# Attention, SoLU and softplus on one core: all later loads of q, k and v issued from ScalarE's queue, under a new order of operations

## The chip, the core and the metric

The kernel runs on one core of a Trainium2 chip. The metric is device microseconds, the median of several executions; lower is better. Instructions are issued by five engines, each in its own program order: TensorE (PE, with PEld for its weight loads), VectorE (DVE), ScalarE (ACT), GpSimd (POOL) and SyncE (SP). SP does no arithmetic: in the kernel before, it issues every transfer between memories.

## The reference

Three stages follow one another. An attention over 4 batches, 8 heads, 576 positions and a head size of 64, where heads 0 to 3 see a window of 32 and heads 4 to 7 see 32 positions at a distance of 4; a first layer of 512 by 1024 by 512 with a SoLU and a normalisation between its two products; a second layer of 512 by 2048 by 512 with a softplus.

```python
scores = scale * np.matmul(q, k.transpose(0, 1, 3, 2))          # masked by window or dilation
attn = softmax(scores);  x = (attn @ v) as [2304, 512]
h = x @ w_in;  solu = h * softmax(h);  ln = (solu - mean) / sqrt(var + 1e-6) * g_ln
x = ln @ w_out
h = x @ w2_in;  out = softplus(h) @ w2_out
```

## The kernel before

All inputs are float32. Most products are made from a float16 high part and a float16 low part of each operand, three products instead of one; weights and activations are therefore split on ScalarE and VectorE (a high part `...h`, a low part `...l` or `...o`) before TensorE can use them.

The attention is cut into 28 pairs of blocks (`pair`, line 886): seven for each batch, of two kinds. The first ten (`NF = 10`, handled by `pair32`) are computed in float32 with their transposes on TensorE. The other eighteen, pairs 10 to 27, which I call the later pairs, are split into float16 parts, and everything that has to be turned is turned by transfers: `qT` and `kT` (q and k), `pT` (the probabilities, needed by the product with v, `PV`), `xT` (the attention output). `lnT` does the same for the normalised rows of the first layer. These transfers are `dma_t`, line 581. The plain loads are `dma`, line 578: a later pair of the dilated kind has three (`ld11.0`, `ld11.1`, `ld11.2` for q, k, v), one of the windowed kind six (`ld10.00`, `ld10.01` for q, `ld10.10`, `ld10.11` for k, `ld10.20`, `ld10.21` for v), 78 for all of them. They go into the buffers `rq`, `rk` and `rv`, which have one to three slots each, some of them lying in the tile `E`. A load can start when the pair that had the slot before has been split (`ql`, `kl`, `vl` on VectorE are the last to read it).

The order of all work is written out. The body of the program creates 2923 operations (`P.op`), each with the engines that may run it (`opts`); the list `ORDER` (line 191) names them in the order in which they are emitted, and `SLOTS` gives each buffer its slot. Every instruction is pinned to that order on its engine (`pin`, line 548). An entry below zero stands for a filler: one matrix product of constants into an idle bank, 512 columns wide, that nobody reads (`mm`, line 569, on the tile `eye`). The engine comes from this line of `order` (line 104):

```python
o.on = next(iter(o.opts)) if len(o.opts) == 1 else "DVE" if x >= n else "ACT"
```

Here `x` is the entry of the list and `n` is 2923. An operation with one possible engine runs there. One with two runs on ScalarE unless its entry has 2923 added to it. At the end of the program the operations are emitted one after the other by `o.fn(o.on)` (line 1883). When ScalarE passes from an exponential to a softplus or back, a load of its function table goes ahead (line 1882).

The pairs overlap with the other stages: by the trace the first layer's product of the first rows (`m1a0`) starts at 47 us, the first hidden product of the second layer (`h0.0`) at 124 us, the last pair ends at about 465 us, and from then on the second layer alone remains.

Of the kernel before, what the change touches and what calls it, by code (L numbers as in the profile page):

```python
# [134 lines left out]
def dma_cost(issue, land):  # L135
    return {"SP": (issue, land)}


def moving(packets, size, lag=2.05):

    return 1.05 * packets * (12 + size / 21.0) / 16000, lag
# [3 lines left out]
def kernel(  # L145
# [12 lines left out]
    nc = tc.nc  # L158
# [4 lines left out]
    HH = H // 2  # L163
# [413 lines left out]
    def dma(out, in_):  # L577
        pin(nc.sync.dma_start(out=out, in_=in_))
# [1335 lines left out]
```

## Time and profile before

| | |
|---|---|
| median of 3 runs | 687.52 us (685.85 to 689.7) |
| the profiled execution | 686.92 us |
| its span, first to last instruction | 685.2 us |
| PE busy | 665.7 us (97%) |
| DVE busy | 616.8 us (90%) |
| ACT busy | 490.5 us (72%) |
| transfers issued by SP | 217 plain, 126 turning |
| fillers in the list | 165 |

A busy PE is not one at its peak: matrix products are pipelined, and fillers count as busy too. The engines' shares are means over stages that differ; the stretches in the rows below tell them apart.

### The profile page before, as it was taken

What the parts mean: (1) busy time and instruction counts of PE and PEld (TensorE: products, weight loads), DVE (VectorE), ACT (ScalarE), POOL (GpSimd) and SP (SyncE); (2) the same over time, 40 slices, a digit from 0 to 9 for tenths busy, and PEclk for the clock granted to TensorE, in tenths of its full rate; (3) what the DMA queues carried; (4) which work ended last, traced back from release to release, by engine and by line L of the source; (5) the groups of instructions that cost most, each with busy time, mean ns of one, the idle gap of its engine ahead of it and who ended that gap; (6) DMA issues with size and microseconds to landing.
All of it is one profiled execution on the core that took longest, in us unless ns stands there. A gap on an engine that the chain in (4) does not pass through costs nothing.

```text
span 685.2 us, 14857 instructions
## 1 busy us (share of the span) xinstructions
PE 665.7 (97%) x5462; PEld 482.0 (70%) x5462; DVE 616.8 (90%) x1770; ACT 490.5 (72%) x1022; POOL 3.5 (1%) x22
## 2 busy tenths in 40 slices
PE   6999999999999999999999999999999999999997
PEld 4666557767875587777567757765758786788886
DVE  4999999999999878888889898888899999998997
ACT  5899998999998678755989669855544255553553
POOL 2000000000000000000000000000000000000000
PEclk9999999999999999999999999999999999999999
DMA  9999997788675669997878887753121200000000
GB/s 269 254 254 257 250 232 187 149 163 192 173 149 142 182 188 202 217 166 143 139 143 154 161 145 153 110 105 74 32 47 27 52 1 1 32 1 2 33 32 32
DMA packets 186776, 89.84 MB, mean 131 GB/s; under 512 B 157000, under 2 KB 174416, under 8 KB 186704
## 3 DMA queue, kind: packets, MB, share of 16 engines
q1 hardware_dynamic: 186704, 88.90, 58.6%
q8 instruction: 43, 0.70, 0.4%
q14 instruction: 29, 0.24, 0.1%
HBM read 54.53 MB, written 4.72 MB: 86 GB/s over the span
## 4 chain that ended last, share of the span: by engine, by line
PE 76%; DVE 9%; DMA 7%; ACT 4%; issue 2%; SPq 1%; DVEq 0%; ACTq 0%
PE bank L569 32%; PE ps_w L569 25%; PE bank L1688 11%; PE ps_w L1605 7%; DMA E<-in_moe_w_in_dram 2%; DVE W L560 2%; DMA pT<-p 2%; PE bank L575 1%; DMA W<-in_moe_w_out_dram 1%; ACT W L551 1%; ACT E L551 1%; DMA W<-in_moe_w_in_dram 1%; DVE osb L560 1%; ACT s L551 1%; DVE E L560 1%
## 5 line engine op out<-in xcount | busy, mean ns | idle before, releaser
L569 PEld LDWEIGHTS <-W 128*128 128x128 f16 x1824 | 176.6, 98 | 24.2 <-DMA lnT<-hl 1.5
L569 PE MATMUL ps_w<-W,g 128*128 128x512 f16 x576 | 130.4, 379 | 0.0
L569 PE MATMUL bank<-y,W 128*128 128x256 f16 x960 | 109.9, 273 | 0.0
L569 PE MATMUL bank<-lnT,W 128*128 128x256 f16 x864 | 98.8, 273 | 1.4 <-DVE rs L566 1.4
L569 PE MATMUL ps_w<-W,xr 128*128 128x512 f16 x432 | 98.0, 379 | 0.0
L569 PEld LDWEIGHTS <-g 128*128 128x128 f16 x576 | 55.4, 98 | 60.5
L569 PEld LDWEIGHTS <-xr 128*128 128x128 f16 x432 | 41.8, 98 | 45.4
L1688 PEld LDWEIGHTS <-W 128*128 128x128 f16 x528 | 51.7, 98 | 7.5
L1882 ACT ACT_TABLE_LOAD x39 | 50.0, 1283 | 0.7
L551 ACT ACTIVATE s<-s 96x128 f32<-96x128 f32 (+3 forms) x144 | 43.6, 374 | 8.7 <-DVE s L557 8.5
L551 ACT ACTIVATE E<-E 128x768 f32<-128x768 f32 (+2 forms) x48 | 35.9, 749 | 12.9 <-DMA E<-in_q_dram 5.1
L560 DVE SCALAR_TENSOR_TENSOR g<-r,KR,g 128x512 f16<-128x512 f32 (+1 forms) x57 | 40.9, 719 | 0.9 <-ACT g L551 0.7
L1136 DVE CUSTOM_DVE_ANT_0 s<-bank,band,bsc 96x128 f32<-96x128 f32 (+3 forms) x144 | 38.9, 323 | 1.7 <-PE bank L569 1.6
L569 PE MATMUL ps_w<-eye 128*128 128x512 bf16 x125 | 34.1, 379 | 0.0
L551 ACT ACTIVATE g<-r,KR 128x512 f16<-128x512 f32 (+1 forms) x41 | 28.2, 690 | 7.3 <-PE ps_w L1605 3.7
L551 ACT ACTIVATE hl<-e,st 128x1024 f16<-128x1024 f32 x18 | 22.3, 1238 | 14.9 <-DVE st L560 11.9
L551 ACT ACTIVATE r<-bank,invC 128x512 f32<-128x512 f32 x40 | 27.1, 684 | 7.8 <-DVE g L560 3.7
L569 PEld LDWEIGHTS <-eye 128*128 128x128 bf16 (+2 forms) x185 | 17.9, 104 | 16.7 <-POOL eye L627 4.0
L569 PEld LDWEIGHTS <-pT 128*96 128x96 f16 (+3 forms) x432 | 22.6, 123 | 7.2 <-DMA pT<-p 3.1
L560 DVE SCALAR_TENSOR_TENSOR E<-E 128x512 int32<-128x512 int32 x40 | 26.9, 684 | 0.2
L1605 PE MATMUL ps_w<-W,g 128*128 128x256 f16 x180 | 25.5, 273 | 0.6 <-DVE osb L560 0.6
L551 ACT ACTIVATE xf<-bank,rs 80x64 f32<-80x64 f32 (+1 forms) x100 | 22.9, 316 | 4.3 <-DVE rs L566 3.9
(368 smaller groups left out, 1306.6 us busy)
## 6 DMA issues: line engine op xcount, KB each, us to landing
E<-in_moe_w_in_dram SPq DMA_DIRECT2D x17, 512.0 KB, 4.8
E<-in_moe_w_out_dram SPq DMA_DIRECT2D x17, 512.0 KB, 4.1
out_dram<-osb SPq DMA_DIRECT2D x18, 256.0 KB, 2.6
W<-in_moe_w_in_dram SPq DMA_DIRECT2D x7, 512.0 KB, 5.6
W<-in_moe_w_out_dram SPq DMA_DIRECT2D x7, 512.0 KB, 4.8
E<-in_v_dram SPq DMA_DIRECT2D x9, 384.0 KB, 4.4
E<-in_q_dram SPq DMA_DIRECT2D x9, 384.0 KB, 4.1
E<-in_k_dram SPq DMA_DIRECT2D x9, 384.0 KB, 4.0
```

Of the source, the lines that this page charges most:

```text
L551: pin(nc.scalar.activation(out=out, in_=in_, func=func, **kw))
L560: pin(nc.vector.scalar_tensor_tensor(out=out, in0=in0, scalar=s, in1=in1, op0=op0, op1=op1, **kw))
L569: pin(nc.tensor.matmul(out, l, r, start=start, stop=stop))
L575: pin(nc.tensor.transpose(out, in_, eye32[:in_.shape[0], :in_.shape[0]]))
L1136: pin(nc.vector.tensor_tensor_reduce(out=sv()[:rows, h, :nk], in0=sb.t[:rows, h, :nk], in1=band[:rows, 48 - m:48 - m + nk], scale=sc[:rows ...
L1605: pin(nc.tensor.matmul(mi[q](), gt.t[:, a, ff, 128 - 128 * t:256 - 128 * t], b(w), start=start and x == 0, stop=x == 2, skip_group_check=True,
L1688: pin(nc.tensor.matmul(ps.t[:, ff, :], at(w, cc, ff), yo.t[:, v, cc, :], start=start, stop=cc == 1 and x == 2, skip_group_check=True,))
L1882: pin(nc.scalar.preload_act_table_set(TABLES[tab]))
```

## The change

Three edits. `dma` gets a third argument and issues on ScalarE's queue when that is "ACT", on SyncE's otherwise. The loads of pairs that are not `whole`, the later pairs, get a second possible engine, "ACT", and pass their engine on. `ORDER` and `SLOTS` are replaced by new lists. Transfers that turn (`dma_t`) and all other loads and stores stay on SyncE's queue.

```diff
     ORDER = (
-        64, 65, 237, -2, 240, 3164, 238, -2, 242, 243, -2, -2, 244, 245, 268, 267, 246, 0, 13, 256, 3, 14, 15, 16,
...
-    def dma(out, in_):
-        pin(nc.sync.dma_start(out=out, in_=in_))
+    def dma(out, in_, eng="SP"):
+        pin((nc.scalar if eng == "ACT" else nc.sync).dma_start(out=out, in_=in_))
...
-                        dma(buf.t[:cnt].rearrange("p (h r d) -> p h r d", h=HH, r=2), s)
+                        dma(buf.t[:cnt].rearrange("p (h r d) -> p h r d", h=HH, r=2), s, e)
...
-                    f"ld{n}.{x}", dma_cost(0.45, 2.35), load, uses=[buf], mv=moving(4 * cnt, 512),
+                    f"ld{n}.{x}", dma_cost(0.45, 2.35) if whole else {**dma_cost(0.45, 2.35), "ACT": (0.45, 2.35)}, load, uses=[buf], mv=moving(4 * cnt, 512),
...
-                        dma(to, s)
+                        dma(to, s, e)
...
-                    two.append(P.op(f"ld{n}.{x}{o}", dma_cost(0.45, 2.35), load, uses=[buf], mv=moving(4 * cnt, 256)))
+                    two.append(P.op(f"ld{n}.{x}{o}", dma_cost(0.45, 2.35) if whole else {**dma_cost(0.45, 2.35), "ACT": (0.45, 2.35)}, load, uses=[buf], mv=moving(4 * cnt, 256)))
```

The change is described as moving sixteen loads. Read from the code it moves 78: with two engines in `opts` a load runs on ScalarE unless its entry is 2923 or more, and no load of a later pair has such an entry in the new list. Counted from the lists: fillers fall from 165 to 148, loads of a function table on ScalarE rise from 39 to 43, and 119 splits and copies that either engine can do change sides, 59 from ScalarE to VectorE and 60 back.

## Rows read from the trace of the kernel before

**Rows 1.** Page, part 1: busy time, share of the span, instructions.
```profile
PE 665.7 (97%) x5462; PEld 482.0 (70%) x5462; DVE 616.8 (90%) x1770; ACT 490.5 (72%) x1022; POOL 3.5 (1%) x22
```

**Rows 2.** Windows: length, then PE, PEld, DVE, ACT, POOL busy, PEclk, DMA share, GB/s.
```profile
25.00:125.00 100.00, 96.56 (x749) 62.16 (x747) 97.67 (x271) 93.69 (x274) 0.00 (x0) 1.00 0.91 233
125.00:250.00 125.00, 123.78 (x966) 85.93 (x964) 116.13 (x341) 112.74 (x227) 0.00 (x0) 1.00 0.73 168
250.00:450.00 200.00, 196.19 (x1733) 141.70 (x1731) 171.00 (x623) 156.00 (x299) 0.00 (x0) 1.00 0.83 157
450.00:675.00 225.00, 224.41 (x1815) 174.61 (x1813) 211.04 (x485) 112.18 (x180) 0.00 (x0) 1.00 0.14 32
...
275.00:300.00 25.00, 24.78 (x219) 18.06 (x218) 20.64 (x79) 16.70 (x33) 0.00 (x0) 1.00 1.00 194
```

**Rows 3.** Waits of PE from 125 to 455 us: total, times, longest.
```profile
PE bank L569 <- DMA kT<-E: 1.4, 1, 1.4
PE bank L569 <- DVE s L1136: 1.3, 2, 1.1
PE bank L569 <- DVE E L560: 1.2, 1, 1.2
PE bank L569 <- DVE xf L563: 0.8, 2, 0.5
PE bank L569 <- DMA pT<-p: 0.3, 1, 0.3
```

**Rows 4.** Chain that ended last, 324 to 340 us: start, length, what.
```profile
328.98 1.07 SPq L581
...
330.21 2.85 DMA pT<-p
...
337.90 0.85 DVE s L1136 x7
```

**Rows 5.** The same chain, 396 to 406 us.
```profile
398.11 2.01 SPq L581
...
400.52 3.68 DMA kT<-E
```

**Rows 6.** Timeline of SP, 324.7 to 350.4 us; 21 transfers in all.
```profile
324.72 1.68 SPq L581 DMA_TRANSPOSE E<-qk  x1
...
328.16 0.57 SPq L578 DMA_DIRECT2D rv<-in_v_dram  x1
...
330.21 1.21 SPq L581 DMA_TRANSPOSE pT<-p  x1
...
335.61 1.90 SPq L578 DMA_DIRECT2D E<-in_v_dram  x1
337.56 1.55 SPq L581 DMA_TRANSPOSE qT<-E  x1
...
349.93 0.50 SPq L578 DMA_DIRECT2D E<-in_q_dram  x1
```

**Rows 7.** Line 578, the plain transfers: ns min/median/max of an issue, first and last.
```profile
L578 SPq DMA_DIRECT2D rk<-in_k_dram x27: 328/480/1227, 1.7 to 401.9; - x27
L578 SPq DMA_DIRECT2D rv<-in_v_dram x19: 378/526/1331, 39.7 to 450.3; - x19
```

**Rows 8.** Timeline of ACT, 147 to 150 us.
```profile
147.76 0.62 ACT L551 ACTIVATE E<-E 128x512 bf16<-128x512 f32 x1
```

**Rows 9.** Chain, 147 to 149 us.
```profile
148.03 0.02 ACTq L551
...
148.50 5.94 DMA E<-in_moe_w_in_dram
```

**Rows 10.** Groups by line: busy us, mean ns, idle before.
```profile
L1882 ACT ACT_TABLE_LOAD x39 | 50.0, 1283 | 0.7
...
L551 ACT ACTIVATE s<-s 96x128 f32<-96x128 f32 (+3 forms) x144 | 43.6, 374 | 8.7 <-DVE s L557 8.5
...
L569 PE MATMUL ps_w<-eye 128*128 128x512 bf16 x125 | 34.1, 379 | 0.0
...
L551 ACT ACTIVATE g<-r,KR 128x512 f16<-128x512 f32 (+1 forms) x41 | 28.2, 690 | 7.3 <-PE ps_w L1605 3.7
```

**Rows 11.** Timeline of PE, 99 to 108 us: fillers, and the end of the front.
```profile
102.50 1.46 PE L569 MATMUL bank<-eye 128*128 128x512 bf16 x6
...
107.11 1.16 PE L569 MATMUL bank<-lnT,W 128*128 128x256 f16 x9 [1.39 <-DVE rs L566]
```

**Rows 12.** Chain, 98 to 126 us.
```profile
98.78 6.04 DMA E<-in_moe_w_in_dram
...
124.13 1.97 PE bank L569 x18
```

383 rows, old and new, of tables (ORDER, SLOTS) are left out of this document.

## The prediction, made before the change was run

> **What bounds the kernel now.** I read the shares of the page first [rows 1]: TensorE is busy 97% of the span, VectorE 90%, ScalarE 72%. These are means over stages, so I went to the stretches [rows 2]. TensorE's granted clock is 1.00, the 2.4 GHz level, in each of them, so no term below is a clock term. From 450 us on TensorE is busy for 224.41 of 225 us with matrix products alone: nothing that the change does can shorten that stage. From 25 to 125 us VectorE (97.67 of 100) and ScalarE (93.69) are both full with splitting weights, the transfer engines stand at 0.91, and TensorE's 96.56 is partly filler. From 250 to 450 us, the stage of the later pairs, VectorE has 171 of 200 us, ScalarE 156, so ScalarE has 44 us free there, but 112.74 of 125 us in the stretch before.
>
> Then the waits of TensorE between 125 and 455 us [rows 3]. They add up to 1.4 + 1.3 + 1.2 + 0.8 + 0.3 = 5.0 us. That is all the plain idle time which a better feed of the later pairs could give back. To see whether SyncE's queue is behind it I followed the chain that ended last. At 328.98 us it goes through 1.07 us in which SyncE is the one that is late, then through the turning of the probabilities (2.85 us to landing) into the softmax work of VectorE at 337.90 us [rows 4]; at 398.11 us it goes through 2.01 us of SyncE and then the turning of k, 3.68 us [rows 5]. The queue is nearly full: from 324.72 to 350.43 us I add up the issues of 21 transfers to 23.2 us of 25.7, 90% [rows 6]. The nine plain loads among them take 7.3 us, 28% of the time; a turning transfer that is ready has to wait for whatever stands before it, and one load alone (335.61 us) stood for 1.90 us. So the direction of the change is right: SyncE's queue limits the turning transfers, and they are on the path.
>
> **The change part by part.** *SyncE loses 78 issues.* At the medians of 480 and 526 ns [rows 7], about 0.5 us each, that is 39 us, of which 57 loads, 28 us, lie after 250 us (counted in the trace). By the chain, 1.4 + 1.3 us of the waits hang on SyncE being late; the 0.8 and 0.3 us wait for probabilities that were turned or for what follows them. The 1.2 us follows VectorE's work on a weight that landed 5.94 us after its issue [rows 9], and stays. So 3.8 us can be reached. I take 2.5 of them, nearer to all than to none, since the loads' 28% of the queue's time comes free, but not all, since the transfers take 2.85 and 3.68 us to land by themselves and the 16 transfer engines are at 0.83 in the mean and 1.00 from 275 to 300 us [rows 2]. Bounds: 0 and 5.0 us.
>
> On that last point the Trainium skill, "DMA: Bandwidth & Descriptors", section "Issuing engines are not separate DMA queues", says that transfers issued by different engines run on the same 16 DMA engines and interleave, and that issuing from several saves only the issue time. By that rule only the two places where the chain names SyncE itself would improve; the trace agrees in so far as the landing takes longer there than the lateness of the queue.
>
> *ScalarE gains 78 issues.* No load is issued by ScalarE in the trace of before, so I bound the cost. From above: each takes 0.5 us of ScalarE as it does of SyncE, 39 us in all, 28 of them after 250 us. From below: nothing, because ScalarE's sequencer goes on while the engine works: at 148.03 us it executes a semaphore instruction [rows 9] in the middle of an operation that runs from 147.76 to 148.38 us [rows 8]. An issue of 0.5 us then lies beside the operation ahead of it, and those take 0.37 us (one head's exponential) to 0.69 us [rows 10]. A gain below nothing is excluded: nothing leaves ScalarE's queue. I take 0.15 us each, near the lower end, because the operations around the loads are mostly of the longer kind: 9 us after 250 us. To this come four more table loads, 4 x 1.283 = 5.1 us [rows 10]. Together 14 us, into 44 us of free time: 0 on the path. If that cover is gone, they cost their full length; that is a rival below. A load that waits for its slot holds every ScalarE operation behind it, the exponentials and splits of the next blocks, and through them VectorE and TensorE. Counted in the new list, 66 of the 73 loads that follow another pair in their slot have at least 1.5 us of VectorE's work between the release and the load, half of them over 8 us; so I price this wait at 0, with up to 1.5 us for seven of them, some 5 us if all fell on the path.
>
> *The front.* By the place of `h0.0` the new list has 16 fillers fewer. Six of them in a row take 1.46 us, so one goes by in (1.46 - 0.38) / 5 = 0.22 us [rows 10, 11], and 16 are 3.5 us. This is no gain by itself: fillers stand where TensorE has nothing else to do. At 107.11 us TensorE waits 1.39 us for VectorE [rows 11], and VectorE for the landing of a weight, 6.04 us after its issue [rows 12]. The bytes to be moved and the work of VectorE, which is full, are unchanged in sum (summed over both lists with the durations of the trace, VectorE's work ahead of the last split before `h0.0` agrees to within 1 us), and seven loads with 3.5 us of issue go to ScalarE, which has 6 us free in this stretch. I take 0, with bounds of 3.5 us less and 3 us more. The second half of the kernel, after 450 us, gets 0: its order changes, but TensorE has no gap to lose.
>
> *Sum.* -2.5 (turning transfers) + 0 (ScalarE) + 0 (front) + 0 (tail) = -2.5 us on the span of 685.2 us, 682.7 us. The profiled execution took 686.92 us, 1.7 us beyond its span, which makes 684.4 us; the median of the runs shown, 687.52 us, is 0.6 us above that execution. So I forecast 685.0 us, 0.4% less.
>
> **The rivals.** *A. ScalarE becomes late (slower).* Each load holds ScalarE's sequencer not for 0.5 us but until SyncE's current transfer has been issued, and the operations behind it run late. In the stretch of 25.7 us the 12 turning transfers take 15.9 us [rows 6], 62% of the time, and one takes 1.2 to 1.7 us. If the two queues issue one at a time, a load is held by up to 1.2 us on top of its own 0.5, and the cover of 0.4 to 0.7 us ahead of it no longer reaches. The point from which this decides: 57 loads share 44 - 5 = 39 us of free time after 250 us, 0.68 us each. At 0.8 us beyond the cover the stage grows by 57 x 0.12 = 7 us and the 2.5 us are not gained either: 694 us. For it speaks that ScalarE is already at 93 to 94 of 100 us in the first stretch and 90% in the second; against it that its sequencer runs ahead [rows 8, 9] and that it has the time.
>
> The skill, "Perfetto Trace Analysis", section "DMA Instruction — HWDGE (DVE, Sync)", says that the unit which generates descriptors is locked for exclusive use by one instruction, that the sequencer waits for the lock, and that the semaphore wait too is served by the sequencer. That is this rival's mechanism. No trace with one issuing queue can show the lock.
>
> *B. The front shortens as well (faster).* If all of the 5.0 us goes and the 16 fillers do mark time that TensorE no longer waits in, 687.5 - 5.0 - 3.5 = 679 us. For it: the chain runs through SyncE in the middle. Against: VectorE's 97.67 of 100 us.
>
> *C. Nothing moves.* The turning transfers still land late, because the transfer engines at 0.83 to 1.00 are the limit and not the queue, and ScalarE covers its issues: 687.5 us, give or take 1. The same comes out if the change did not do what it says; if only sixteen loads moved, SyncE would lose a fifth of the 39 us, and the gain would be 0.5 us.
>
> **How the numbers follow.** My forecast has a chance of 0.42 and a range of its own of 682 to 688 us. A has 0.27, B 0.16, C 0.15. Half a per cent, 3.4 us, is about what a measurement of this kernel can tell from no change: below 684.1 is faster, above 691 slower. Of the forecast 0.17 falls below 684.1 and 0.25 within; B is all faster; C within but for 0.01; A slower but for 0.02. That makes faster 0.33, same 0.41, slower 0.26. For 8 in 10 the range must take in most of A and half of B: 680 to 693.5 us, leaving out about 0.08 below and 0.1 above.
>
> **What the profile of the changed kernel would show.** Right: 78 issues on ScalarE's queue of about 0.5 us, most of them while an operation of ScalarE runs; SyncE no longer in the chain between 300 and 450 us; waits of TensorE between 125 and 455 us of about 2.5 us; ScalarE at 165 to 175 of 200 us in the stretch 250 to 450. For A: issues on ScalarE of over 1 us, idle time of ScalarE ended by "issue" or by its own queue, and waits of TensorE and VectorE for exponentials and splits. For B: `h0.0`, now at 124.13 us [rows 12], before 121 us. For C: the same waits, now for transfers alone. The prediction is wrong if an issue on ScalarE costs more than 0.68 us beyond its cover, if the front moves by more than 3 us either way, or if the new order opens gaps after 450 us.

## The result, and the profile after

The changed kernel takes 697.0 us in the median (695.3 to 698.2), the kernel before beside it 687.5: 1.0140 times as long, with an interval of 1.0116 to 1.0164, or 9.6 us. The forecast was 685.0 us, its range ended at 693.5. The profiled execution took 696.4 us with a span of 693.2. I follow the loss by the starts of the same operations in both traces.

The page after, busy time and transfer queues (packets, MB, share of 16 engines' span; q1 is SyncE's, q10 ScalarE's):

```profile
PE 666.6 (96%) x5445; PEld 481.2 (69%) x5445; DVE 617.6 (89%) x1769; ACT 497.2 (72%) x1042; POOL 3.5 (1%) x22
...
q1 hardware_dynamic: 151792, 77.43, 51.2%
q10 hardware_dynamic: 34912, 11.47, 8.6%
```

The change does what it says, and more than the sixteen loads of its name: 78 transfers, 11.47 MB, are on ScalarE's queue. ScalarE works 6.7 us longer than before [rows 1], of which four more table loads are 5.1; the other engines work as long as before, and TensorE, which ends last, is not kept by more work. The time is in waits.

The windows of after, columns as in [rows 2]:

```profile
25.00:125.00 100.00, 93.07 (x701) 58.57 (x699) 93.54 (x264) 89.19 (x262) 0.00 (x0) 0.97 0.86 224
...
105.00:110.00 5.00, 3.32 (x12) 1.36 (x13) 5.00 (x19) 5.00 (x20) 0.00 (x0) 0.56 0.94 212
110.00:115.00 5.00, 5.00 (x38) 4.01 (x37) 3.50 (x11) 2.99 (x9) 0.00 (x0) 0.75 0.46 131
125.00:250.00 125.00, 119.07 (x913) 80.61 (x913) 114.01 (x340) 109.44 (x220) 0.00 (x0) 1.00 0.76 160
250.00:450.00 200.00, 197.21 (x1736) 143.75 (x1733) 174.25 (x617) 158.98 (x308) 0.00 (x0) 1.00 0.88 163
450.00:675.00 225.00, 224.53 (x1820) 173.78 (x1818) 207.77 (x478) 118.30 (x199) 0.00 (x0) 1.00 0.16 33
```

Beside [rows 2] TensorE is busy 3.5 us less up to 125 us, 4.7 us less from 125 to 250, 1.0 us more in the stage of the later pairs, and as long as before behind 450 us. Busy time counts fillers, and 16 of them fewer are 3.5 us by the prediction's own price, so the first figure is no measure of a delay. The two windows from 105 to 115 us were, before:

```profile
105.00:110.00 5.00, 3.61 (x32) 2.83 (x31) 5.00 (x15) 4.86 (x15) 0.00 (x0) 1.00 1.03 261
110.00:115.00 5.00, 5.00 (x40) 3.41 (x39) 4.54 (x16) 3.35 (x11) 0.00 (x0) 1.00 0.41 120
```

The granted clock there, 1.00 before, is 0.56 and 0.75 after: part of that stretch at the lower level, 1.2 GHz. By the starts of operations the kernel is 4.3 us late at `h0.0` (128.26 us against 123.97), 9.2 us late at the matrix product for the weights of quarter 2 (191.07 against 181.90), and 8.2 us late from 438 us to the end.

The waits of TensorE after, 125 to 455 us (total, times, longest), beside [rows 3]:

```profile
PE bank L569 <- DMA qT<-qk: 3.7, 1, 3.7
PE bank L569 <- DMA kT<-qk: 1.4, 1, 1.4
PE bank L569 <- ACT r L551: 1.0, 2, 0.6
PE bank L569 <- ACT E L551: 1.0, 2, 0.8
PE bank L569 <- DMA pT<-p: 0.8, 2, 0.5
```

With 0.6 us more for `xf` that is 8.5 us instead of 5.0, and turning transfers lead the list. The chain that ended last shows the same places (start, length, what):

```profile
101.67 7.54 DMA lnT<-hl
109.25 4.35 PE bank L569 x24
...
136.71 8.10 DMA qT<-qk
...
153.33 8.79 DMA qT<-qk
162.16 3.79 PE bank L569 x42
170.34 8.50 DMA kT<-qk
```

Before, no turning transfer stood in the chain for more than 3.7 us where I had read it [rows 4, 5], nor for more than 5.0 elsewhere, and none at all between 95 and 205 us; here four take 7.5 to 8.8 us from issue to landing. (Standing in the chain is not a loss by itself: in e1 below, which loses next to nothing, turning transfers stand there for 24.1 us between 95 and 205 us.) What goes on beside the last of them is in the timelines of SP and ACT, 166 to 174 us:

```profile
169.03 1.26 SPq L581 DMA_TRANSPOSE qT<-qk  x1
170.34 2.60 SPq L581 DMA_TRANSPOSE kT<-qk  x1
```

```profile
169.74 0.39 ACTq L578 DMA_DIRECT2D rk<-in_k_dram  x1
171.77 0.45 ACTq L578 DMA_DIRECT2D rk<-in_k_dram  x1
172.37 1.00 ACTq L578 DMA_DIRECT2D rq<-in_q_dram  x2
```

The four loads of pair 13 go out on ScalarE's queue beside the two turnings of pair 12: the first 0.7 us behind that of q, the last within 3 us behind that of k, for which TensorE waits 1.4 us. (The wait of 3.7 us is for the turning of q at 153.33 us.) In the kernel before, three of these four loads stood behind both turnings in SyncE's queue (166.66 to 167.76 us, the turnings at 162.23 and 163.55), and the turnings landed after 3.7 and 4.2 us.

### The profile page after: what moved, and what is told of

It is laid out like the page before. It is cut to its first block, busy times and chain, and to the rows that moved or that the text cites. A ratio compares the mean times of both kernels' runs of the same rounds, so it can differ in the third digit from the quotient of the medians.

```text
span 693.2 us, 14857 instructions
## 1 busy us (share of the span) xinstructions
PE 666.6 (96%) x5445; PEld 481.2 (69%) x5445; DVE 617.6 (89%) x1769; ACT 497.2 (72%) x1042; POOL 3.5 (1%) x22
## 3 DMA queue, kind: packets, MB, share of 16 engines
q10 hardware_dynamic: 34912, 11.47, 8.6%
## 4 chain that ended last, share of the span: by engine, by line
PE 69%; DMA 14%; DVE 8%; ACT 7%; issue 2%; ACTq 0%; SPq 0%; DVEq 0%
PE bank L569 27%; PE ps_w L569 23%; PE bank L1688 10%; PE ps_w L1605 8%; DMA pT<-p 3%; DMA qT<-qk 2%; DVE W L560 2%; DMA E<-in_moe_w_out_dram 2%; DMA rq<-in_q_dram 1%; ACT E L551 1%; DMA kT<-qk 1%; DMA lnT<-hl 1%; DMA E<-in_v_dram 1%; DMA W<-in_moe_w_out_dram 1%; PE bank L575 1%
## 5 line engine op out<-in xcount | busy, mean ns | idle before, releaser
L551 ACT ACTIVATE E<-E 128x768 f32<-128x768 f32 (+3 forms) x49 | 36.4, 743 | 11.0 <-DMA E<-in_q_dram 3.1
L560 DVE SCALAR_TENSOR_TENSOR g<-r,KR,g 128x512 f16<-128x512 f32 (+1 forms) x53 | 37.9, 718 | 3.0 <-ACT g L551 2.8
L569 PE MATMUL ps_w<-eye 128*128 128x512 bf16 x117 | 32.7, 387 | 0.0
L551 ACT ACTIVATE xf<-bank,rs 80x64 f32<-80x64 f32 (+1 forms) x120 | 27.4, 315 | 3.7 <-DVE rs L566 3.5
L569 PE MATMUL bank<-kT,qT 128*80 128x112 f16 (+7 forms) x336 | 22.7, 235 | 5.2 <-DMA qT<-qk 3.7
L569 PEld LDWEIGHTS <-eye 128*128 128x128 bf16 (+2 forms) x168 | 16.4, 105 | 15.5 <-POOL eye L627 4.0
```

What stands on the lines that cost most here:

```text
L551: pin(nc.scalar.activation(out=out, in_=in_, func=func, **kw))
L560: pin(nc.vector.scalar_tensor_tensor(out=out, in0=in0, scalar=s, in1=in1, op0=op0, op1=op1, **kw))
L569: pin(nc.tensor.matmul(out, l, r, start=start, stop=stop))
```

## The experiments

Three theories. **Contention**: on a queue of their own the loads run beside the turning transfers on the same 16 transfer engines, and these land later. **Order**: the new list costs the time, whatever queue the loads are on. **ScalarE**: the issue holds ScalarE (rival A). The kernel before ran beside each kernel; "+" is the ratio's excess times 687 us.

| run | median us | ratio, 95% interval | us |
|---|---|---|---|
| changed list, all loads on SyncE (e1) | 687.0 | 0.9996 to 1.0045 | +1.4 |
| old list, all 78 on ScalarE (e2) | 692.2 | 1.0059 to 1.0111 | +5.8 |
| old list, pairs 10 to 13 on ScalarE (e6) | 693.5 | 1.0080 to 1.0127 | +7.1 |
| old list, pairs 14 to 27 on ScalarE (e4) | 687.9 | 1.0003 to 1.0039 | +1.4 |
| old list, pairs 10 to 13 on ScalarE, half of each load (h2) | 689.9 | 1.0021 to 1.0070 | +3.2 |
| old list on SyncE, 78 small issues on ScalarE (e5) | 687.7 | 0.9997 to 1.0029 | +0.9 |
| changed, five loads back on SyncE (e8) | 690.7 | 1.0038 to 1.0092 | +4.5 |
| changed, pairs 10 to 13 back on SyncE (a1) | 688.7 | 1.0007 to 1.0070 | +2.6 |
| changed, once more, two executions (a2) | 695.7 | 1.0085 to 1.0197 | +9.7 |

**Order or queue.** e1 keeps the changed list and undoes the queue; e2 keeps the old list and does the queue alone.

```
e1   def dma(out, in_, eng="SP"):
-        pin((nc.scalar if eng == "ACT" else nc.sync).dma_start(out=out, in_=in_))
+        pin(nc.sync.dma_start(out=out, in_=in_))
e2   dma(), load and options as in the changed kernel; ORDER and SLOTS of the kernel before
```

> The changed list with all 78 loads issued on SyncE again, so that only the order differs from the kernel before. Three theories. Order: the new list by itself loses the time (later weight loads, fewer fillers, clock at 0.50 near 105 to 112 us), whatever queue the loads are on: 695 to 699 us, h0.0 near 128 us, and the PE wait of 3.7 us on qT near 160 us still there. Contention: loads on a second queue run beside the turning transfers and make these land later: 689 to 692 us, because the losses after 128 us (about 5 us) go and only the first 4.3 us stay; the median landing of qT between 125 and 205 us goes back from 7.6 us to about 5.8. ScalarE: holding ScalarE for the issue costs the time: 689 to 692 too, but with the landing times unchanged.

> The order of the kernel before, with all 78 loads of q, k and v of pairs 10 to 27 on ScalarE's queue, so that only the queue differs from the kernel before. Order: no loss, 685 to 688 us, the PE waits of 125 to 455 us at 2.5 to 5.0. Contention: 691 to 696 us, qT's median landing between 125 and 205 us near 7.6 us instead of 5.8 and PE waits of several us on qT and kT there, h0.0 still near 124. ScalarE: 691 to 696 with landings as before and ScalarE's idle time ended by issue.

The changed list on SyncE takes 687.0 us and cannot be told from the kernel before: the order by itself costs at most 3.1 us (1.0045), and the order theory falls. The old list with the loads on ScalarE loses 5.8 us; its `h0.0` is 3.3 us late, where I had expected it near 124 us. Between e1 and the changed kernel only the queue differs, and that is 8.2 us. The waits of TensorE in e1, 125 to 200 us, have the 3.7 us on `qT` down to 0.8 and none on `kT`:

```profile
PE bank L569 <- DMA qT<-qk: 0.8, 1, 0.8
PE bank L569 <- ACT E L551: 0.7, 1, 0.7
```

I had expected e1 at 689 us or more, with the first 4.3 us of loss left in it; it had 2.0 at `h0.0` and gave them back later.

**ScalarE.** e5 lets ScalarE issue 78 transfers of 32 bytes where e2 had the loads, which stay on SyncE.

```
     pin(nc.sync.dma_start(out=out, in_=in_))
+    if eng == "ACT":
+        r = next(taken_rows)
+        pin(nc.scalar.dma_start(out=scratch[r:r + 1, :], in_=q[0, 0, r:r + 1, 0:8]))
```

> The kernel before, unchanged in order and with all loads on SyncE, and beside it 78 small transfers of 32 bytes on ScalarE's queue at the places in the list where the old-list run had the loads: ScalarE pays the issues, next to no bytes move. ScalarE theory (holding ScalarE costs the time): 690 to 693 us, as the old list with the loads on ScalarE (692.2). Contention theory (the loads' own packets beside the turning transfers cost it): 686 to 688.5 us, the turning transfers landing as in the kernel before.

```profile
L582 ACTq DMA_DIRECT2D scratch<-in_q_dram x78: 208/209/1161, 40.0 to 451.7; - x78
```

The issues (the row gives ns min/median/max) cost 0.9 us, 2.0 at the end of the interval; e2 lost 5.8 with as many issues and the bytes. These issues are shorter than a load's; three of the loads' groups in the changed kernel's trace are:

```profile
L578 ACTq DMA_DIRECT2D rv<-in_v_dram x19: 319/391/1187, 40.4 to 435.7; - x19
L578 ACTq EVENT_SEMAPHORE  x19: 17/17/3745, 95.1 to 418.3; - x19
L578 ACTq DMA_DIRECT2D rk<-in_k_dram x18: 319/386/516, 95.2 to 411.1; - x18
```

So a load holds ScalarE's sequencer for 0.39 us, less than the 0.48 and 0.53 us on SyncE [rows 7]. One load of 78 waited for its slot, 3.7 us at 313.1 us; ScalarE stood idle for 3.3 us behind it, and TensorE didn't wait there. Rival A falls as the cause of the 9.6 us; that issues as long as a load's cost a little more than e5's is not excluded.

**Which loads.** e6 and e4 split the old list's 78 loads; a1 and e8 take loads of the changed kernel back to SyncE at the same places. (An entry of the list above 2922 selects an operation's second option, for a load SyncE.)

```
e6, e4   ORDER of before, with entry -> entry + 2923 for the loads that stay on SyncE
a1       ORDER of after, entry -> entry + 2923 for the 18 loads of pairs 10 to 13
e8       1210 -> 4133, 1273 -> 4196, 1274 -> 4197, 1275 -> 4198, 1276 -> 4199
```

> The order of the kernel before, with the loads of pairs 10 to 13 alone on ScalarE's queue and those of pairs 14 to 27 on SyncE: the complement of the run with the late pairs, which lost 1.5 us. If the losses add up and lie mostly in the stretch where weight loads fill the engines, 690 to 691.5 us (4.4 us lost), lnT1 landing in over 7 us and the clock falling near 105 to 115 us; the stretch from 250 us on as before. If the loss is spread over all loads alike (22 of 78 here), 688 us.

> The order of the kernel before, with the loads of pairs 14 to 27 alone on ScalarE's queue, pairs 10 to 13 still on SyncE. Nothing ahead of about 200 us changes. Contention that costs only where SyncE's queue is full of weight loads and turning transfers: the front as before, the middle stage (250 to 450 us) 1.0 to 2.5 us shorter, 685 to 686.5 us. Contention that costs everywhere: pT and kT between 285 and 460 us land 0.4 to 1.0 us later and the time is 688 to 690 us. ScalarE: 688 to 692 us with ScalarE's busy share in 250 to 450 us at 165 or more of 200. Order alone: 687 us, no change.

> The changed kernel with the loads of pairs 10 to 13 (22) on SyncE at the same places of the list, those of pairs 14 to 27 still on ScalarE. Contention: all loads on SyncE took 687.0 us, all on ScalarE 697.0; the old list lost 7.0 us by the early loads and 1.5 by the late ones, the spliced list 2.75 by the late ones, so 688.5 to 690 us here, and 7 to 8.5 of the 10 us come back. If the late loads cost the changed list as much as the early ones: 692 us.

> The changed kernel with five of its 78 loads (ld12.1 and the four of pair 13 that follow qT12 and kT12) issued on SyncE at the same places of the list. Contention theory: qT11 (landing 8.8 us) and kT12 (8.5 us) were late because these loads ran beside them; the losses between 150 and 195 us (about 5 us) go, w2o2m begins 4 to 5 us late instead of 9.2, and the time is 691.5 to 693.5 us. If the turning transfers are late there for another reason (the weight loads ahead of them on SyncE): 696 to 698 us. ScalarE theory: five issues fewer, 0.3 us at most, 696 to 697 us.

Pairs 10 to 13 have 18 loads, six for each of the two windowed pairs and three for each of the two dilated; the expectations of a1 and h2 say 22, which is a miscount. These 18 early loads carry the loss: +7.1 alone on the old list (693.5 us, where I had expected 690 to 691.5), and taken back they bring the changed kernel from +9.6 to +2.6. Five of them make 5.1 of these 7.0. The 60 late ones cost 1.4 us, where I had hoped for a gain of 1.0 to 2.5. The parts don't add up exactly (7.1 + 1.4 against 5.8 for both). The intervals of e6 and e2 overlap; that a delay made early takes up part of one made later would also do it, and is not shown. In e8 the waits of TensorE from 125 to 200 us are:

```profile
PE bank L569 <- DMA qT<-qk: 1.5, 1, 1.5
PE bank L569 <- ACT E L551: 0.6, 1, 0.6
```

The wait on `kT` is gone with the four loads of pair 13, that on `qT` is down by 2.2 us with the one load (`ld12.1`) that had gone out 0.17 us behind it. What happens shows best at `kT10`, whose neighbours `ld11.1` and `ld11.0` went out 0.05 to 0.5 us behind it on ScalarE's queue. Transfers issued around it (KB, us to landing) in e6, then in a1:

```profile
rk<-in_k_dram ACTq DMA_DIRECT2D x1, 224.0 KB, 7.0
rq<-in_q_dram ACTq DMA_DIRECT2D x1, 160.0 KB, 9.0
kT<-qk SPq DMA_TRANSPOSE x1, 9.5
```

```profile
rk<-in_k_dram SPq DMA_DIRECT2D x1, 224.0 KB, 3.6
kT<-qk SPq DMA_TRANSPOSE x1, 4.4
```

In the six profiles with these loads on ScalarE that give its landing `kT10` lands after 7.5 to 9.5 us, in the ten with them on SyncE after 4.4 to 6.6 (old list 9.2 and 9.5 against 5.0 to 6.6, changed list 7.5 to 8.7 against 4.4 to 5.5). `lnT1` likewise: 7.5 (changed), 8.5 and 8.6 (e2, e6) against 5.7 to 6.4 (e7, e1, a1). The loads land later too, as the lines show. It is not that one queue lets the turning go first: in all ten the load of k stands 0.38 us ahead of `kT10` in SyncE's queue, that of q 1.3 to 1.9 us behind it and the next weight, 512 KB, 2.1 to 2.6 us behind. With the loads on ScalarE's queue the load of k goes out 0.05 us behind the turning, that of q 0.4 to 0.5 and the weight 1.3 us. So two queues put more in flight beside the turning, sooner. Which of these neighbours makes it late no run here separates.

That both queues' packets are served side by side is in e6's queues from 134.0 to 144.5 us (packets, MB, share of 16 engines):

```profile
q1 hardware_dynamic: 1774, 1.42, 82.5%
q10 hardware_dynamic: 800, 0.39, 24.4%
```

The Trainium skill, "DMA: Bandwidth & Descriptors", section "Queues, rings and completion order", says that each transfer engine takes turns between the queues that have work for it, packet by packet. The trace agrees that both move at once; no run here shows the size of a turn.

**Half the bytes.** If it is the bytes, half of them should cost half. h2 leaves out the second half of the partitions of each of these 18 loads, and with them half of the packets.

```
     if eng == "ACT":
+        half = out.shape[0] // 2
+        out, in_ = out[:half], in_[:half]
```

> The order of the kernel before with the loads of pairs 10 to 13 on ScalarE's queue, as in the run that took 693.5 us, but each of these 22 loads brings only the first half of its partitions (the other half of the tile keeps what an earlier load left, so half of q, k and v of these pairs is not loaded anew). If the loads' packets beside the turning transfers cost the 7 us: about half comes back, 689 to 691 us, kT10's landing between 6 and 8 us and lnT1's near 7. If a second queue costs per transfer, whatever its size: 692.5 to 694 us, kT10 at 9 us, lnT1 at 8.5 us.

+3.2 us instead of +7.1, with as many transfers: the cost goes with what the transfers carry, bytes or packets, and not with their number, as in e5. This holds for the time as a whole. In the profile the front still lost nearly as much as in e6 (w2i1 4.0 us late against 4.7), and 2 of the 3.5 us between the two kernels' ends lie behind 182 us; so in the front itself it is not shown. The trace gives no landing of `kT10` in this run.

**The fillers.** Two kernels put 15 back ahead of `ya0.1` (e3 in the changed kernel, e7 in e1), three take them from the kernel before (b1 17, b2 the 10 between PV8.0 and PV8.1, b3 the 7 ahead of w2i1).

```
e3, e7   ORDER: + -1 x4 ahead of tx7.0, -1 x2 of PV8.1, -5 x3 of tx8.0, -5 x6 of ya0.1
b2       ORDER of before: - the four -1 ahead of tx7.0, the six -1 ahead of tx7.1
b3       ORDER of before: - the seven -5 ahead of w2i1m      (b1: both)
```

> The changed kernel with 15 filler matmuls more, 4 ahead of tx7.0, 2 ahead of PV8.1, 3 ahead of tx8.0 and 6 ahead of ya0.1, where TensorE stood idle 0.98, 0.63 and 1.28 us. If the fall of the granted clock to 0.50 behind those gaps is what the second loss is made of, the clock stays at 1.00, ya0.1 takes 2.7 us instead of 4.35 and the time falls by 1.5 to 2.2 us, to 695 us. If the clock only follows a wait that is there anyway (lnT1 lands at 109.2 us, and the weights after it late), h0.0 stays at 128 us and the time at 696 to 697 us.

> The changed list with all loads on SyncE and the 15 fillers put back ahead of ya0.1. The list alone stood 2.0 us behind at h0.0, with the clock at 0.68 in 105 to 115 us, and won 3.2 us behind 250 us. If the clock is what costs it the front: 684.5 to 685.5 us, clock 1.00 through 105 to 115 us, h0.0 at most 1 us late. If lnT1's landing and the weight loads cost it: 686.5 to 687.5 us, no change.

> The kernel before without 17 of its fillers (10 between PV8.0 and PV8.1, 7 ahead of w2i1m), all loads on SyncE: the front's fillers as the changed list has them, nothing else moved. If fillers hold up the clock there and the clock sets h0.0: the granted clock falls below 0.9 in 100 to 115 us, ya0.1 takes over 4 us instead of 2.8, h0.0 begins 1.5 to 2.2 us later and the time is 688 to 689 us. If fewer fillers cost nothing (the forecast's front term of zero): clock 1.00 or the delay taken up before h0.0, 686 to 687 us.

> The kernel before without the 10 fillers between PV8.0 and PV8.1 alone. The run without 17 took 690.1 us (1.0019 to 1.0079 times the kernel before), but its profiled execution was its fastest and lost only 0.4 us in the front. If the clock's fall behind that gap is the price: clock under 0.9 in 100 to 115 us and 688 to 690.5 us. If the fillers there are free: 685.5 to 687 us.

> The kernel before without the 7 fillers ahead of w2i1m alone, which stand behind ya0.1 and yb0.1. If the clock's fall belongs to the gap ahead of ya0.1: clock 1.00 in 100 to 115 us and 685.5 to 687 us. If these seven carry the cost of the 17: 688 to 690.5 us.

| run | median us | ratio, 95% interval | clock in 105 to 110, 110 to 115 us |
|---|---|---|---|
| e3 | 693.3 | 1.0072 to 1.0142 | 1.00, 1.00 |
| e7 | 688.1 | 1.0008 to 1.0042 | 1.00, 1.00 |
| b1 | 690.1 | 1.0019 to 1.0079 | 0.66, 1.00 |
| b2 | 688.3 | 1.0008 to 1.0056 | 0.92, 0.50 |
| b3 | 688.0 | 0.9981 to 1.0034 | 1.00, 1.00 |

b2's windows from 105 to 115 us:

```profile
105.00:110.00 5.00, 2.41 (x26) 2.09 (x25) 5.00 (x21) 5.00 (x17) 0.00 (x0) 0.92 0.94 214
110.00:115.00 5.00, 5.00 (x25) 3.30 (x25) 5.00 (x15) 4.99 (x17) 0.00 (x0) 0.50 0.59 171
```

Without the ten fillers TensorE stands idle for 2.6 of 5 us and the clock is at the lower level in the 5 us behind; beside the kernel before, b2 loses 1.5 us between `w2o0` and `w2i1` (its profiled execution, 695.3 us, was its longest and had lost 5.3 us ahead of 50 us already, which no filler touches), and it is 0.3% slower in all. In b1's profile, its fastest execution (686.8 us), the same ten are gone and the clock is 0.66 in 105 to 110 us, yet nothing is lost between these two places. Without the seven behind `yb0.1` nothing is told apart. So the ten at that place are worth 0.5 to 3.8 us (1.0008 to 1.0056). What they are worth in the changed list stays open: 15 more brought the changed kernel from 1.0140 to 1.0107, but the intervals overlap, and on SyncE they brought nothing: e7 took longer than either of its two expectations, and its `h0.0` was 2.7 us late with the clock at 1.00, e1's 2.0.

**The later pairs alone.** Both lists have done the same operations after their 1133rd, near 205 us, so they can be joined there: the old front with the changed rest, on SyncE (s1) and with the loads of pairs 14 to 27 on ScalarE (s2).

```
s1, s2   ORDER = before[up to the 1133rd operation] + after[from there]; SLOTS to match
```

> The list of the kernel before up to its 1133rd operation (about 205 us; both lists have done the same operations there), the changed list behind it, all loads on SyncE. The changed list on SyncE stood 2.4 us behind at 205 us and 0.4 to 0.8 us ahead from 420 us on, in one profile. If that gain of 3.2 us belongs to the changed order of the middle: 683 to 684.5 us. If it was only slack that took up an earlier delay: 686 to 687.5 us, no change.

> The same spliced list with the loads of pairs 14 to 27 on ScalarE's queue: the change with its front left as it was. The forecast's own term (turning transfers land 2.5 us earlier in all when the loads leave SyncE) gives 683.5 to 684.5 us and pT and kT between 285 and 460 us landing no later than on SyncE. Contention gives the spliced list on SyncE plus 1 to 2.5 us, 685 to 687 us, with pT at 3.5 us or more instead of 3.0 to 3.2.

s1 takes 687.9 us (1.0013 to 1.0046), s2 690.7 (1.0041 to 1.0088). The changed rest by itself wins nothing: what e1 had won back behind 250 us (3.2 us in its profile) looks like slack that takes up an earlier delay. In s1 the same stretch first falls 3.1 us behind (223 to 266 us) and then wins 2.9 back. And on ScalarE's queue the late loads cost 2.4 us more in this list, though the queue was all that the forecast's gain rested on. The medians from issue to landing, 285 to 460 us, in the changed kernel and then in e1:

```profile
pT<-p SPq DMA_TRANSPOSE x25, 4.0
lnT<-hl SPq DMA_TRANSPOSE x4, 5.3
```

```profile
pT<-p SPq DMA_TRANSPOSE x25, 3.2
lnT<-hl SPq DMA_TRANSPOSE x5, 4.5
```

With the queue freed, these turning transfers take 0.8 us longer from issue to landing. That they are issued sooner is not in these numbers, but it wins nothing on balance. In s2 against s1 it is `lnT` (5.4 against 4.4) and hardly `pT` (3.4 and 3.3), so which transfer is late changes with the list.

**The same kernel again.** a2 tells which delays of the first profile repeat.

> The changed kernel once more, for a second profile of it: which of its delays are the same in two executions. The first had h0.0 4.3 us late, w2o2m 9.2 us late and 8.2 us at the end. If the front's delay is a property of the kernel: h0.0 3.5 to 5 us late again. If it is chance that every kernel has there (kernels alike up to 150 us showed 1.8 to 4.3 us): between 1.5 and 3.5 us, with the end the same within 1.5 us.

`h0.0` was 2.2 us late this time instead of 4.3, `w2o2` 8.5 instead of 9.2, the end 7.1 instead of 8.2. The waits on `qT` and `kT` between 125 and 200 us are there again:

```profile
PE bank L569 <- DMA qT<-qk: 4.0, 1, 4.0
PE bank L569 <- DMA kT<-qk: 1.1, 1, 1.1
```

So some 2 us of the front's delay is chance of an execution, and what is lost between 150 and 191 us, 5.1 and 6.5 us in the two, is the firm part. No kernel here beats the kernel before.

## Why the prediction was wrong, point by point

*What bounds the kernel.* That SyncE's queue is full and stands in the chain [rows 4 to 6] was right, and the conclusion drawn from it was not. The transfer engines behind it were busy for 0.73 to 0.91 of the time [rows 2]; a second queue beside the first made no room on them.

*SyncE loses 78 issues: -2.5 us, bounds 0 and 5.0.* This is the step that failed. I let the landing time of a turning transfer be what it was before and bounded the term at 0, as though a transfer on another queue could do it no harm. e2 puts the queue by itself at +5.8 us (4.1 to 7.6), e6 and h2 show that it goes with what the loads carry while they move beside the turnings, and e5 that it is not the issue. The forecast also looked only at the stage behind 250 us. Of the 78 loads 18 go out before about 205 us, in a stretch where the engines also carry 512 KB weight transfers, and those 18 make 7.0 of the 9.6 us. I had the waits from 125 us on in [rows 3] and none of them was a turning transfer before 250 us; I did not ask what would make one there. The rule that I quoted from the Trainium skill ("DMA: Bandwidth & Descriptors", section "Issuing engines are not separate DMA queues": the same 16 engines, interleaved, only the issue time saved) put the gain at the two places where the chain names SyncE. The traces agree that the transfers share the engines; e1 against the changed kernel shows that the second queue costs 8.2 us here, where that rule has a small gain.

*ScalarE gains 78 issues: 0.* Right. 0.34 to 0.50 us by the medians of the groups, at most 1.19; e5 gives +0.9 us with 0 inside the interval; one load waited 3.7 us for its slot, more than the 1.5 us allowed for each, and off the path; ScalarE is busy for 158.98 of 200 us between 250 and 450, less than the 165 to 175 I expected. The four table loads came (43 instead of 39) and show nowhere as a wait of TensorE.

*The front: 0, from -3.5 to +3.* Measured +4.3 and +2.2 at `h0.0` in two profiles. First, the step above fails here too: with every filler in place the loads on ScalarE's queue put `h0.0` 3.3 (e2) and 4.7 us late (e6), with `lnT1` landing after 8.5 and 8.6 us and the clock at 0.68 and 0.66 between 110 and 115 us. Kernels with the front of the kernel before, loads on SyncE, were up to 1.8 us late there in their profiles, which I take for chance. Second, "fewer fillers are no gain by itself" together with "no term is a clock term": I asked whether dropping fillers wins time and not whether it loses any. In the old list the clock of 1.00 [rows 2] was kept up by ten of them: without those it falls to the lower level (b2), and 0.5 to 3.8 us are lost. That the fillers matter in the changed list is not shown (e7 and e1).

*The tail: 0.* Right: 8.2 us late at 438 us and at 632 us.

*The rivals.* A had the right side and 694 us, for a reason that the runs exclude: no group of issues on ScalarE's queue reached the 0.68 us in the median, and e5 pays 78 shorter ones for 0.9 us. That its time lies near the measured one is luck. The rule of the Trainium skill behind it ("Perfetto Trace Analysis", section "DMA Instruction — HWDGE (DVE, Sync)": one instruction at a time has the unit that makes descriptors) would have held a load until SyncE's turning was issued. The trace does not agree: a load was issued in 0.35 us at 153.50 us, while SyncE's issue of `qT11` ran from 153.33 to 154.59, and the 43 loads of 78 that start during the issue of a turning take 0.39 us in the median, as the others do. C named the transfer engines as the limit, which the landings bear out, and priced it at no change; its chance belonged to a slower case. B did not come. The change does move all 78 loads.

*What would show.* Issues of 0.5 us: 0.39. SyncE out of the chain between 300 and 450 us: this came, 3.9 us of the chain before and 0.02 after, and none in e2 and e4. The gain that was to follow did not. Waits of 2.5 us: 8.5. Behind 250 us alone they fell, from 3.8 to 2.6 us, but the changed list on SyncE has 1.2 there (e1), and the old list with its late loads on ScalarE 4.8 (e4); so by these profiles the fall is the list's and not the queue's. Front moved by more than 3 us: yes in one profile of two. That was the sign named for a wrong prediction.

## What to carry to other kernels

A second queue issues sooner, but here it brought no transfer engines of its own: bulk loads moved to it went out beside the short transfers that the path waits for, and both landed later. A sign such as the full queue leaving the chain can come true without the gain. Before splitting a queue, look at the share of the transfer engines and at what will go out in the same 3 us as each transfer on the path, in every stretch where a moved load lies, not only in the one meant to gain. And price a dropped filler from both sides: ten whose loss brought the granted clock down cost 0.5 to 3.8 us, seven without which it stayed at 1.00 nothing that could be told.

## What was not expected of the hardware

- Five loads, 672 KB in all (224, twice 128 and twice 96), on the second queue instead of the first cost 5.1 us (e8 against the changed kernel). The two turnings beside them landed after 8.8 and 8.5 us; in the kernel before the same two took 6.6 and 3.7.
- A load was issued faster on ScalarE's queue than on SyncE's (medians of 0.39 against 0.53 us for v, 0.39 against 0.48 for k).
- The issue of a turning transfer on SyncE is normally 1.2 us for `pT` but took 3.32 us at 155.41 us; while it ran, 17 packets of 256 or 512 bytes that began between 156.58 and 157.75 us took 1.0 to 2.1 us each (18 ns is the median of those of 256 bytes), and all ended near 158.7 us, with the issue. The same is in the kernel before at 148.90 us (2.93 us, packets of up to 2.8 us), so it is no effect of the second queue. Its cause was not looked for.
